# Attention and two MoE layers on one core: a buffer of its own for the scaled last weight, the softmax reciprocals through the landing buffers, and another order of the planned work

## The chip, the cores and the metric

One core of a Trainium2 chip runs the whole program. The metric is the device time of one execution in microseconds (us), and each number for a kernel is the median of several executions.

The five engines of the core go by short names: PE is TensorE (matmuls; PEld are its weight loads), DVE is VectorE, ACT is ScalarE, POOL is GpSimd and SP is SyncE, which here only issues DMAs. A DMA issued by SP or POOL waits in that engine's instruction queue, in order, until the buffer that it writes is free; the transfer itself then runs beside the engines.

## The reference

Attention over 4 batches, 12 heads, 448 positions and head size 64, whose output goes through two dense layers:

```python
scores = cap * np.tanh(q @ k.T / sqrt(64) / cap)          # per batch and head
attn   = exp(scores - max) / (sum + 1e-9)
x      = (attn @ v)                                        # -> [1792 tokens, 768]
h      = ((x @ w1) * (x @ w2)) @ w3 @ w_out                # 768 -> 1024 -> 1024 -> 768
h      = h @ w_in                                          # second layer, 768 -> 1024
solu   = h * softmax(h);  ln = (solu - mean) / sqrt(var + 1e-6) * g_ln
out    = ln @ w_out2                                       # 1024 -> 768
```

## The kernel before

**Arithmetic.** Operands are split into a high and a low part (`split`: ACT copies the high part, DVE subtracts), and a product is three matmuls. The weights arrive as 64-bit words: SP loads a piece into a landing buffer (`landing`, tag `ld`, three of them), and `convert` turns it into 32-bit numbers with three DVE instructions, L168 to L170, into one of two buffers with the tag `cv`.

**Stages.** While attention runs (24 pairs of heads), PE is given other matmuls between the attention's. First is the fold: w3 times w_out (L375), then that times w_in (L393), stored to `w_dr` and loaded back in 16 pieces through the landing buffers (`load34`). Then come the gated products `ab` (L601), w1 and w2 of the first layer against the attention's results `xs`, for batches 0 and 1, and after attention's end for batches 2 and 3. From 582 us on there are two stages of block products (`seven`, L731): the folded matrix, then the last weight `wout2` against the second layer's activations.

**The planned work beside it.** Everything that feeds these matmuls stands in one list (`Ahead`, filled in order by `plan_...`). An item has up to three steps: a load, a first step and a rest; loads run up to three items ahead, and two items are taken for each half pair of heads. The items that matter here:

- `plan_w(f)`, f from 0 to 7: three pieces of w1 and w2, landed, converted and split into `wt`, of which there are two at a time. The slot for f is free when the products of f - 2 are done.
- `plan_last(f)`: two halves of the last weight. Each is landed and converted into a `cv` buffer, scaled in place by `g_ln` on ACT (L532) and stored from that buffer to `wg_dr` by SP (L533).
- `plan_x(b)`: three parts of two head pairs each. POOL loads the reciprocals of the softmax sums, spread over 64 partitions each, into the one buffer `rb` (L456); DVE multiplies the attention's output `xr` by it (L464); `split` makes `xs` of that. There are three `xr` buffers, and part (b, i) uses the buffer of part (b - 1, i).

The list's order before is w0, x of batch 0, w1, x of batch 1, w2, w3, then w4 to w7 each followed by four halves of the last weight, and the x of batches 2 and 3 behind all that. A scheduler then orders each engine's instructions from this: the list sets priority and, among loads that want a landing buffer, who gets it; work whose own buffers are free may run much earlier than its place in the list. At the end of each pair, ACT copies the outputs out of PSUM (L303, two buffers `x`), and POOL moves them into `xr` (L304).

Of the kernel before, what the change touches and what calls it, by code (L numbers as in the profile page):

```python
# [10 lines left out]
F32 = mybir.dt.float32  # L11
F32R = mybir.dt.float32r
U32 = mybir.dt.uint32
AF = mybir.ActivationFunctionType
# [5 lines left out]
P = 128  # L20
B, H, S, D = 4, 12, 448, 64
NPAIR = H // 2
NT = B * S
DM = H * D
DF = 1024
NC, NF = DM // P, DF // P
HALF = 512
# [12 lines left out]
LANDS = 3  # L40
# [5 lines left out]
def raw(ap):  # L46

    return ap.bitcast(F32)
# [50 lines left out]
def attention_moe_solu(ctx: ExitStack, tc: tile.TileContext, q, k, v, cap, w12, w3t, wo, win, wout2, g_ln, out):  # L99
# [9 lines left out]
    pe, act, dve, pool, sync = nc.tensor, nc.scalar, nc.vector, nc.gpsimd, nc.sync  # L109
# [18 lines left out]
    gt = const.tile([P, NF], F32, name="gt")  # L128
    conv = ctx.enter_context(tc.tile_pool(name="conv", bufs=1))
# [18 lines left out]
    lands, cvs = {}, {}  # L148

    def landing(i, src, n, kind):  # L150
        t = conv.tile([P, 2 * HALF], U32, tag="ld", bufs=LANDS, name=f"ld{i}")
        lands[i] = t[:, :n].bitcast(kind)
        dst = lands[i]
        if len(src.shape) == 3:
            dst = dst.rearrange("p (a b) -> p a b", a=src.shape[1])
        elif len(src.shape) == 4:
            dst = dst.rearrange("p (a b c) -> p a b c", a=src.shape[1], b=src.shape[2])
            for g in range(src.shape[1]):
                sync.dma_start(out=dst[:, g], in_=src[:, g])
            return  # L160
        sync.dma_start(out=dst, in_=src)

    def convert(i, n):

        d = lands.pop(i).rearrange("p (n w) -> p n w", w=2)
        lo, hi = d[:, :, 0], d[:, :, 1]
        x = conv.tile([P, HALF], U32, tag="cv", bufs=2, name=f"cv{i}")[:, :n]
        dve.tensor_scalar(x, hi, 5, 2, ALU.logical_shift_left, ALU.logical_shift_right)  # L168
        dve.scalar_tensor_tensor(x, hi, 0xC0000000, x, ALU.bitwise_and, ALU.bitwise_or)  # L169
        dve.scalar_tensor_tensor(x, lo, 29, x, ALU.logical_shift_right, ALU.bitwise_or)  # L170
        cvs[i] = x.bitcast(F32)

    def split(th, tl, x):
        act.copy(th, x)
        dve.tensor_tensor(tl, x, raw(th), ALU.subtract)  # L175
# [11 lines left out]
    landed, ready, parts, outs, xr, stored, inv = {}, {}, {}, {}, {}, set(), [None]  # L187
# [215 lines left out]
    wt, xs, rb, fin = {}, {}, {}, set()  # L403
# [14 lines left out]
    def plan_w(f):  # L418
        for i in range(3):
            plan64(("w", f, i), w12[f, i], HALF, lambda i=i: slot12(f, i), lambda: free12(f))  # L420

    def plan_again(f):
        def load():
            for i in range(3):
                slot12(f, i)
            sync.dma_start(out=raw(wt[f]), in_=w12_dr[f - NF])
        for i in range(3):
            ahead.add(("w", f, i), load if i == 0 else (lambda: None), lambda: None, lambda: None, None, lambda: free12(f))

    def place_x(b, c):  # L430

        n = b * NC + c
        if n < W3 or n >= 2 * W3:
            return w3p.tile([P, 2, HALF], F32R, tag="w3", bufs=W3, name=f"xs{b}_{c}")[:, :, :S]
        return place["x"].tile([P, 2, S], F32R, tag="xs", bufs=W3, name=f"xs{b}_{c}")

    def free_x(b, part):
        if (b, part) not in stored:
            return False
        if b == 0:  # L440
            return pos[0] >= STAGE1 + (HALFWAY if part else 0)
        return (pos[0] >= STAGE1 + HALFWAY if (b, part) == (1, 0) else "x" in place) and (b < 3 or (NF - 1, 0) in fin)

    def plan_x(b):
        for part in range(NPAIR // 2):
            if (b, part) == (B - 1, NPAIR // 2 - 1):

                plan_again(NF + 2)
            i = len(ahead.items)
            pairs = slice(2 * part, 2 * part + 2)  # L450

            def load(i=i, pairs=pairs):
                rb[i] = conv.tile([P, 2, S], F32, tag="rb", name=f"rb{i}")
                for j in range(2):
                    row = r_dr[b].rearrange("(n j) s -> j n s", j=2)[j:j + 1, pairs]
                    pool.dma_start(out=rb[i][j * D:(j + 1) * D], in_=row.to_broadcast([D, 2, S]))  # L456

            def first(i=i, part=part):

                for c in (2 * part, 2 * part + 1):  # L460
                    xs[b, c] = place_x(b, c)
                one = raw(xs[b, 2 * part + 1][:, 0, :1])
                pool.memset(one, 1.0)
                dve.scalar_tensor_tensor(xr[b, part], xr[b, part], one, rb.pop(i), ALU.mult, ALU.mult)  # L464

            def rest(part=part):
                x = xr.pop((b, part))
                for i in range(2):
                    split(xs[b, 2 * part + i][:, 0], xs[b, 2 * part + i][:, 1], x[:, i])
            ahead.add(("x", b, part), load, first, rest, None, lambda part=part: free_x(b, part))  # L470
# [55 lines left out]
    def plan_last(f):  # L526
        for u in range(2):
            i = len(ahead.items)

            def rest(i=i, u=u):  # L530
                t = cvs.pop(i)
                act.activation(t, t, AF.Copy, scale=gt[:, f:f + 1])  # L532
                sync.dma_start(out=wg_dr[f, u], in_=t)  # L533
            ahead.add(("g", f, u), lambda i=i, u=u: landing(i, wout2[f, u].bitcast(U32), DM, U32), lambda i=i: convert(i, DM // 2), rest)

    plan_w(0)
    plan_x(0)
    plan_w(1)
    plan_x(1)
    for f in range(2, NF):  # L540
        plan_w(f)
        if f >= 4:
            plan_last(2 * f - 8)
            plan_last(2 * f - 7)
    plan_again(NF)
    plan_again(NF + 1)
    plan_x(2)
    plan_x(3)
    for i_ in range(NF // 2):
        for part in range(2):  # L550
# [124 lines left out]
    for s in range(2 * NP + 1):  # L675
        n, u = divmod(s, 2)
# [149 lines left out]
    w, wg = DM // 2, {}  # L826
# [102 lines left out]
```

## Time and profile before

| | us |
|---|---|
| median of three runs | 840.35 (839.52 to 841.06) |
| the profiled execution, its own time | 839.32 |
| its span, first to last instruction | 837.5 |
| PE busy | 819.4 (98%) |
| DVE busy | 596.7 (71%) |
| ACT busy | 482.9 (58%) |
| POOL busy | 77.5 (9%) |
| mean granted TensorE clock | 0.993 |

The profile is of one execution. Starts are microseconds from the first instruction. A wait is idle time of an engine just ahead of an instruction, with what ended it. Matmuls overlap and their ends are modelled, so the busy share of PE flatters it a little; what counts is how closely the matmuls follow one another.

### The profile page before, as it was taken

How to read it: one execution, taken by the hardware profiler on the slowest of the kernel's cores; microseconds unless marked ns; L12 is line 12 of the kernel's file. 1: busy time of each engine (PE TensorE's matmuls, PEld its weight loads, DVE VectorE, ACT ScalarE, POOL GpSimd, SP SyncE). 2: the span in 40 equal slices, each digit the busy share in tenths (PEclk: the TensorE clock that was granted, in tenths of full speed). 3: DMA queues.
4: the chain of work that ended last, by engine and by line, in shares of the span. 5: the costliest groups of instructions: out<-in, count | busy, mean ns of one | idle time of the engine just before them, and what ended most of it. 6: DMA issues, size and time to landing. Idle time of an engine off the chain costs nothing.

```text
span 837.5 us, 12335 instructions
## 1 busy us (share of the span) xinstructions
PE 819.4 (98%) x4392; PEld 686.6 (82%) x4392; DVE 596.7 (71%) x1068; ACT 482.9 (58%) x745; POOL 77.5 (9%) x147
## 2 busy tenths in 40 slices
PE   6999999999999999999899999999999999999998
PEld 4677898667677787777778899999888888999997
DVE  7999986896866688786883554342987876995452
ACT  4698866698787676766762121112555655863341
POOL 1012001112111111011112000000000000000000
PEclk8999999999999999999999999999999999999999
DMA  8777775777786366668679699992533325744211
GB/s 262 261 222 224 225 212 176 215 256 249 233 244 189 83 231 220 209 218 279 213 231 295 215 368 390 359 330 73 191 101 126 101 101 189 228 184 155 88 64 75
DMA packets 92573, 173.48 MB, mean 207 GB/s; under 512 B 9696, under 2 KB 63200, under 8 KB 90464
## 3 DMA queue, kind: packets, MB, share of 16 engines
q1 hardware_dynamic: 87520, 161.51, 57.8%
q0 software_dynamic: 4992, 11.19, 5.3%
q8 instruction: 34, 0.56, 0.3%
q14 instruction: 27, 0.22, 0.1%
HBM read 116.40 MB, written 50.68 MB: 199 GB/s over the span
## 4 chain that ended last, share of the span: by engine, by line
PE 62%; DMA 11%; DVE 11%; issue 10%; ACT 5%; POOL 1%; SPq 0%; DVEq 0%; ACTq 0%; POOLq 0%
PE ab L601 21%; PE u L731 16%; PE v L731 8%; PE o L286 5%; PE y L731 4%; PE f L393 3%; DVE cv L170 2%; PE sc L245 2%; DVE cv L169 2%; ACT sc L254 2%; DMA inv<-x 1%; PE tp L801 1%; DMA ld<-w_dr 1%; DMA wg_dr<-cv 1%; DMA ld<-in_wo 1%
## 5 line engine op out<-in xcount | busy, mean ns | idle before, releaser
L601 PE MATMUL ab<-xs,wt 128*128 128x448 f32 x1152 | 242.4, 369 | 1.5 <-DMA wt<-w_dr 0.9
L601 PEld LDWEIGHTS ab<-xs,wt 128*128 128x128 f32 x1152 | 216.2, 189 | 25.5 <-issue 6.1
L286 PE MATMUL o<-hi,v 128*66 128x448 f32 (+1 forms) x396 | 95.3, 371 | 0.9 <-ACT x L303 0.9
L255 ACT ACTIVATE p<-sc,capt 128x896 f32<-128x896 f32 x96 | 87.8, 921 | 12.0 <-DVE lo L270 9.9
L254 ACT ACTIVATE sc<-sc,qscale 128x896 f32<-128x896 f32 x96 | 84.4, 884 | 14.6 <-PE sc L245 13.3
L270 DVE TENSOR_TENSOR lo<-p,hi 128x896 fp32r<-128x896 f32 x66 | 71.4, 1084 | 17.5 <-ACT hi L266 17.5
L731 PE MATMUL u<-ws,a 128*128 128x512 f32 x336 | 82.1, 394 | 0.0
L375 PEld LDWEIGHTS f<-w,w_o 128*128 128x128 f32 x576 | 72.8, 191 | 9.8 <-issue 5.1
L375 PE MATMUL f<-w,w_o 128*128 128x256 f32 x576 | 78.8, 288 | 0.8 <-DVE w_o L175 0.3
L731 PEld LDWEIGHTS u<-ws,a 128*128 128x128 f32 x336 | 62.9, 187 | 14.7
L393 PE MATMUL f<-w_i,w 128*128 128x512 f32 x288 | 71.7, 397 | 0.7 <-DVE w L175 0.4
L266 ACT CAST hi<-p 128x896 fp32r<-128x896 f32 x66 | 62.1, 946 | 11.5 <-PE o L286 11.3
L393 PEld LDWEIGHTS f<-w_i,w 128*128 128x128 f32 x288 | 52.8, 188 | 16.2 <-issue 2.8
L731 PE MATMUL u<-wg,c 128*128 128x384 f32 x336 | 65.4, 340 | 0.0
L286 PEld LDWEIGHTS o<-hi,v 128*66 128x66 f32 (+1 forms) x396 | 42.8, 135 | 26.5 <-issue 10.1
L605 ACT COPY a<-ab 128x448 f32<-128x448 f32 x32 | 17.1, 534 | 74.8 <-PE ab L601 68.4
L731 PEld LDWEIGHTS u<-wg,c 128*128 128x128 f32 x336 | 58.3, 188 | 0.1
L168 DVE TENSOR_SCALAR cv<-ld 128x512 uint32<-128x512 uint32 (+1 forms) x80 | 32.4, 408 | 32.2 <-DMA wg_dr<-cv 13.5
L169 DVE SCALAR_TENSOR_TENSOR cv<-ld,cv 128x512 uint32<-128x512 uint32 (+1 forms) x80 | 52.2, 658 | 0.8
L170 DVE SCALAR_TENSOR_TENSOR cv<-ld,cv 128x512 uint32<-128x512 uint32 (+1 forms) x80 | 52.2, 658 | 0.7
L304 POOL DMA_DIRECT2D xr<-x x48 | 27.5, 576 | 267.8 <-ACT x L303 267.4
L286 PE MATMUL o<-lo,v 128*66 128x448 f32 x132 | 47.6, 365 | 0.0
(129 smaller groups left out, 1228.3 us busy)
## 6 DMA issues: line engine op xcount, KB each, us to landing
ld<-in_w SPq DMA_DIRECT2D x24, 512.0 KB, 4.7
w_dr<-wt SPq DMA_DIRECT2D x8, 1536.0 KB, 7.3
wt<-w_dr SPq DMA_DIRECT2D x8, 1536.0 KB, 8.5
ld<-in_w3t SPq DMA_DIRECT2D x16, 512.0 KB, 4.2
ab_dr<-abs SPq DMA_DIRECT2D x32, 224.0 KB, 5.2
ldab<-ab_dr SPq DMA_DIRECT2D x14, 512.0 KB, 3.9
c_dr<-e SPq DMA_DIRECT2D x14, 512.0 KB, 2.7
ldc<-c_dr SPq DMA_DIRECT2D x14, 512.0 KB, 3.7
```

What stands on the lines that cost most here:

```text
L168: dve.tensor_scalar(x, hi, 5, 2, ALU.logical_shift_left, ALU.logical_shift_right)
L169: dve.scalar_tensor_tensor(x, hi, 0xC0000000, x, ALU.bitwise_and, ALU.bitwise_or)
L170: dve.scalar_tensor_tensor(x, lo, 29, x, ALU.logical_shift_right, ALU.bitwise_or)
L254: act.activation(sc[:, :w, :S], sc[:, :w, :S], AF.Tanh, scale=qscale)
L255: act.activation(p, sc[:, :w, :S], AF.Exp, scale=capt)
L266: act.copy(hi, p)
L270: dve.tensor_tensor(lo, p, raw(hi), ALU.subtract)
L286: product_.append(pe.matmul(outs[n, j][:v_.shape[-1], :S], v_, t[rows, j if c < 3 else 0], **flags))
L375: pe.matmul(f[:, :QW], lw[:, a], rw[:, e], start=(g == 0 and m == 0), stop=(g == NF - 1 and m == 2))
L393: pe.matmul(f, w34[:, a, c, :], rw[:, e], start=(c == 0 and m == 0), stop=(c == NC - 1 and m == 2))
L601: pe.matmul(pp[f, b, i][:, :S], w[:, u], xs[b, c][:, e], start=(c == 0 and m == 0), stop=(c == NC - 1 and m == 2))
L731: pe.matmul(bank, a[m][:, x, k * P:(k + 1) * P], wb[m][:, e, k, :], start=(first and k == 0 and i == 0), stop=(k == NF // 2 - 1 and i == 2 ...
```

## The change

Three things change. The scaled half of the last weight is written by ACT into a buffer of its own (tag `wg`, two of them) and stored from there. The reciprocals land in a landing buffer (tag `ld`) in place of `rb`, which is gone. And the list is put in another order: halves of the last weight stand behind each w from w2 on (w2 g0, w3 g1, w4 g2, w5 g3, w6 g4 g6, w7 g5 g7, where g is `plan_last`), and the three parts of batch 2's x stand behind w4, w5 and w6.

```diff
-    def plan_x(b):
-        for part in range(NPAIR // 2):
+    def plan_x(b, parts=range(NPAIR // 2)):
+        for part in parts:
...
             def load(i=i, pairs=pairs):
-                rb[i] = conv.tile([P, 2, S], F32, tag="rb", name=f"rb{i}")
+                rb[i] = conv.tile([P, 2 * HALF], U32, tag="ld", bufs=LANDS, name=f"rb{i}")[:, :2 * S].bitcast(F32).rearrange("p (n s) -> p n s", n=2)
...
             def rest(i=i, u=u):
-                t = cvs.pop(i)
-                act.activation(t, t, AF.Copy, scale=gt[:, f:f + 1])
+                t = conv.tile([P, DM // 2], F32, tag="wg", bufs=2, name=f"wg{f}_{u}")
+                act.activation(t, cvs.pop(i), AF.Copy, scale=gt[:, f:f + 1])
                 sync.dma_start(out=wg_dr[f, u], in_=t)
...
     for f in range(2, NF):
         plan_w(f)
-        if f >= 4:
-            plan_last(2 * f - 8)
-            plan_last(2 * f - 7)
+        plan_last(f - 2)
+        if f >= 6:
+            plan_last(f)
+        if 4 <= f < 7:
+            plan_x(2, (f - 4,))
     plan_again(NF)
     plan_again(NF + 1)
-    plan_x(2)
     plan_x(3)
```

## Rows read from the trace of the kernel before

**Rows 1.** The page's head: span, then busy time, share and instructions by engine.
```profile
span 837.5 us, 12335 instructions
PE 819.4 (98%) x4392; PEld 686.6 (82%) x4392; DVE 596.7 (71%) x1068; ACT 482.9 (58%) x745; POOL 77.5 (9%) x147
```
**Rows 2.** Busy time by stretch: bounds, length, engines (instructions), granted clock, DMA share, GB/s.
```profile
160.00:240.00 80.00, 78.20 (x388) 56.30 (x388) 64.03 (x105) 64.59 (x92) 10.86 (x20) 1.00 0.80 253
400.00:420.00 20.00, 18.67 (x93) 15.03 (x95) 15.96 (x27) 14.43 (x21) 2.79 (x5) 0.91 0.74 242
480.00:560.00 80.00, 80.00 (x398) 74.44 (x397) 35.75 (x77) 15.10 (x21) 0.00 (x0) 1.00 1.04 367
```
**Rows 3.** PE's waits, 340 to 480 us: total us, times, longest.
```profile
PE sc L245 <- ACT p L255: 2.7, 2, 2.5
PE ab L601 <- DMA wt<-w_dr: 0.9, 1, 0.9
PE ab L601 <- ACT a L605: 0.6, 1, 0.6
```
**Rows 4.** Timeline, 388 to 402 us: start, length, engine, line, operation, [idle before <- releaser].
```profile
390.41 0.36 DVE L168 TENSOR_SCALAR cv<-ld 128x384 uint32<-128x384 uint32 x1 [3.88 <-DMA wg_dr<-cv]
...
392.00 0.62 ACT L532 ACTIVATE cv<-cv,gt 128x384 f32<-128x384 f32 x1 [3.89 <-DVE cv L170]
...
401.33 0.47 PE L245 MATMUL sc<-ql,kh 64*128 64x448 f32 x2 [2.46 <-ACT p L255]
```
**Rows 5.** All engines' waits, 340 to 480 us.
```profile
ACT cv L532 <- DVE cv L170: 24.0, 9, 3.9
...
DVE cv L168 <- DMA wg_dr<-cv: 13.5, 9, 3.9
```
**Rows 6.** The tensor wg_dr: engine, operation, count, duration ns, starts; then landing times.
```profile
L533 SPq DMA_DIRECT2D wg_dr<-cv x16: 319/382/1243, 347.4 to 451.2; - x16
...
DMA to landing us min/median/max: 3.3/5.9/9.2
```
**Rows 7.** Stretches as in rows 2, the gated products' instructions alone.
```profile
402.60:406.10 3.50, 3.31 (x9) 2.96 (x10) 0.00 (x0) 0.00 (x0) 0.51 0.95 278
413.20:416.70 3.50, 3.50 (x18) 3.25 (x18) 0.00 (x0) 0.00 (x0) 1.00 0.88 339
```
**Rows 8.** Line L456, the reciprocals' loads: durations, starts, landing times.
```profile
L456 POOL DMA_DIRECT2D rb<-r_dr x24: 587/604/693, 60.0 to 467.1; - x24
...
DMA to landing us min/median/max: 3.3/4.6/9.3
```
**Rows 9.** Timeline, 143 to 188 us: the first x part, and the outputs that need its buffer.
```profile
144.75 1.14 DVE L464 SCALAR_TENSOR_TENSOR xr<-xr,xs,rb 128x896 f32<-128x896 f32 x1
...
154.56 0.54 POOL L304 DMA_DIRECT2D xr<-x  x1
...
187.64 0.96 ACT L303 COPY x<-o 65x448 f32<-65x448 f32 x2
```
**Rows 10.** Timeline, 175 to 184 us: landing buffers change hands while the fold runs.
```profile
175.98 0.33 SPq L161 DMA_DIRECT2D ld<-in_w  x1
...
176.58 0.33 SPq L161 DMA_DIRECT2D ld<-w_dr  x1
...
180.54 0.84 ACT L174 CAST w<-ld 128x768 fp32r<-128x768 f32 x1 [0.32 <-DMA ld<-w_dr]
...
182.88 0.95 DVE L175 TENSOR_TENSOR w<-ld,w 128x768 fp32r<-128x768 f32 x1
```
**Rows 11.** All engines' waits, 160 to 262 us: those on the landing buffers' loads.
```profile
ACT w L174 <- DMA ld<-w_dr: 7.7, 4, 4.4
DVE cv L168 <- DMA ld<-in_w: 7.7, 4, 2.5
```
**Rows 12.** Timeline, 341 to 366 us: w4's split, and the first output for batch 3.
```profile
341.10 1.15 ACT L174 CAST wt<-cv 128x512 fp32r<-128x512 f32 x2 [0.38 <-PE ab L601]
...
365.51 1.05 POOL L304 DMA_DIRECT2D xr<-x  x2 [2.10 <-ACT x L303]
```

## The prediction

> **What bounds the kernel now.** I read the page's head first: PE is busy for 819.4 of 837.5 us [rows 1], so a change that adds and removes no matmul can only win back PE's gaps or open new ones. The busy time by stretch says where gaps are. From 480 us on PE has none, 80.0 of 80.0 us [rows 2], so a microsecond that PE loses or saves before that is a microsecond of the whole. While attention runs it has a few: 1.8 us in 160 to 240, 1.3 us in 400 to 420 [rows 2]. In that second stretch the granted clock is 0.91 as well, so some of its matmuls ran at the lower of the two levels.
>
> PE's own waits from 340 to 480 us name the gaps where the last weight is prepared [rows 3]: 2.5 us once for an Exp on ACT, 0.6 us for a copy on ACT, 0.9 us for the load of a first-layer weight. The timeline follows the first one back [rows 4]. At 390.41 DVE begins the conversion of a half of the last weight after 3.88 us of waiting for a store to `wg_dr`; at 392.00 ACT begins the scaling of that half after 3.89 us of waiting for the conversion. Both engines work in order, so the Tanh and Exp of scores that were already there stood behind that on ACT, and at 401.33 PE starts new scores after an idle 2.46 us. Nor is it one accident: DVE waited nine times for such a store, 13.5 us in all, and ACT nine times for such a conversion, 24.0 us [rows 5].
>
> **The buffer of its own.** Scaled in place, a `cv` buffer stays taken until its store has landed, 5.9 us in the median and up to 9.2 [rows 6], and there are two. With `wg` it is free when ACT has read it. No instruction is added: ACT's scaling and SP's store have the same sizes and counts, at the same cost. What goes is DVE's 13.5 us of waiting and most of ACT's 24.0; they count only through PE. There I take the 2.46 us [rows 4], the copy's 0.6 us [rows 3], which I put down to the same queueing on ACT, and the slow clock behind the first gap: from 402.6 to 406.1 it was 0.51, with 9 matmuls where a later stretch of the same length has 18 [rows 7], so 3.5 x (1 - 0.51) = 1.7 us. Together 4.8 us; from below the bound is 0, if other waits of the same chain end there. The load's 0.9 us stays: it starts when the last products of batch 1 give up its slot, whatever the rest does.
>
> The change adds a wait: ACT's write of `wg` waits for the store two halves earlier, and behind it on ACT stand the attention's Tanh and Exp. Up to f = 5 the new order has two halves per weight, and the next two only after another weight's slot has come free, so the stores are done. Behind w6 and w7 stand four halves each, so four writes can meet a store under way. The nearest price is DVE's own wait, 13.5 / 9 = 1.5 us [rows 5]. I take 0, because ACT comes to the buffer one conversion later than DVE came to its own; the upper end is 4 x 1.5 = 6.0 us on ACT, of which PE sees a part.
>
> **The other places in the list.** Halves begin behind w2 in place of w4, so the same 16 conversions lie over a longer stretch; cost nothing, as w2 and w3 wait there for their slots anyway. Batch 2's x stands behind w4, w5 and w6. Before, it was far behind in the list and still ran early, as soon as its reciprocals were there. Now its first part comes after w4, whose pieces are split from 341.1, and after two halves; with 4.6 us of landing [rows 8] and 1.1 us of multiplication [rows 9] I put its end at about 356. The next user of its `xr` buffer is POOL's move of batch 3's first output at 365.51 [rows 12]; behind that move on POOL stand the sums' moves and further reciprocals. Nine microseconds cover it, so 0; if they were gone, ACT's output copies would come to wait.
>
> **The landing buffers.** This is what the change pays. `rb` was free, so the first reciprocals were loaded at 60.0 [rows 8] and multiplied at 144.75, long before their place in the list. Now all twelve parts stand in the ring of three landing buffers, in the list's order: the first behind the last piece of w0, loaded at 175.98, the next three before and behind w1. The twelve pairs of POOL loads, their sizes and the twelve multiplications are unchanged; what moves is the time, by some 35 us for the first part.
>
> Two things hang on it. The `xr` buffer of batch 1's first outputs comes free later: POOL's moves of 154.56 shift to about 187, and the copies at 187.64 [rows 9], which can't be made until those moves have landed, by some 3 us. And the fold's pieces stand in the same ring and are needed at once. The piece loaded at 176.58 is split at 180.54, 0.32 us after ACT began to wait for it, and its subtraction ends at 183.8 [rows 10]; that buffer now goes to the reciprocals first. ACT waited 7.7 us for such pieces from 160 to 262 us, and DVE as long for pieces of w1 and w2 [rows 11]: the ring is full.
>
> No row shows reciprocals in a landing buffer. By the piece of 176.58 a buffer is held for 7.2 us, of three, so each of the four parts shifts the ring by 2.4 us: 9.6 us for the last of the fold's pieces, if PE has nothing else. From below it is 0, if attention's matmuls fill PE. A gain is excluded here: a buffer is taken away and none given. Between these I go by this stretch: 7.7 us of ACT's waiting for pieces stood beside 1.8 us of PE idle [rows 2, 11], so 0.23 of a delay reaches PE: 9.6 x 0.23 = 2.2 us.
>
> A rule speaks against the move too. The Trainium skill (SBUF — State Buffer, "SBUF: two separate sides") says that a DMA issued by POOL cannot write its descriptors while certain DVE instructions hold a port that the two share, and gives 3.1 us in place of 0.62 for such a DMA. The reciprocals' loads now fall into a stretch where DVE is busy for 64 of 80 us [rows 2]. By the page, four loads longer by 2.5 us would, as an estimate, add 4 x 2.5 / 3 x 0.23 = 0.8 us. The trace doesn't bear that out: 24 such issues took 587 to 693 ns [rows 8], with DVE as busy.
>
> **The sum.** The profiled execution took 839.32 us, 1.8 more than its span. 839.32 - 4.8 + 2.2 = 836.7 us. The median of the runs shown lies 1.0 above it, so I forecast 837.7 us.
>
> **Rivals.** *The wait moves to ACT* (chance 0.23). One of the four writes behind w6 and w7 meets its store, and a gap like the one at 401 comes back there, without the slow clock: 840.35 - 4.8 + 2.5 + 2.2 = 840.2 us. For it speaks that four halves in a row are what ended so before; against it, that ACT has a conversion's time more.
>
> *The fold starves* (0.29). PE's idle follows the ring in full, between 176 and 235 us: 840.35 - 4.8 + 9.6 = 845.2 us. It decides from the point where over 6.5 of the 9.6 us reach PE (4.8 won plus the 1.7 us that can be told from no change). For it: PE works ACT and DVE hard there, 64.6 and 64.0 of 80 us [rows 2], so attention can't run ahead freely. Against it: PE hid most of such delays so far. A worse form is in this chance: reciprocals ready at 60.0 would take a landing buffer then and hold it until 144.75; the list's order should keep that from happening.
>
> **How the numbers follow.** The forecast's case has 0.48, with its own range of 835.6 (nothing lost in the ring) to 838.6. Two executions of this kernel differ by about 0.2%, 1.7 us, and no less can be told from no change. By the cases: faster 0.48, same 0.23, slower 0.29. The range goes from 834.0, for small gaps beyond the three that I counted, to 845.2, the starved fold's.
>
> **What would show it.** Right: DVE's waits for stores of `wg_dr` gone, ACT's waits for conversions of these halves well under 24.0 us, no PE gap over 1 us between 340 and 460 us and a clock of 1.00 there; the first multiplication by reciprocals near 182; PE idle in 160 to 240 us at about 4 us in place of 1.8. Wrong: a gap of the same kind after 410, with ACT waiting for a store; PE idle of over 8 us in 160 to 240; or a fold whose early loads, before 144 us, come later than now. A scheduler orders all of it anew, so single gaps may move for reasons that none of these steps holds.

## The result, and the profile after

The kernel after takes 845.58 us in the median (842.30 to 846.72), the kernel before, run beside it, 839.90 us (838.02 to 841.68). The ratio is 1.007, with a 95% interval of 1.0052 to 1.0088: slower, where faster was forecast. The time lies 0.4 us above the top of the range. It is the time of the rival "the fold starves", 845.2 us, and most of what follows asks how far its reason was the right one. In the code of after the lines from 543 on stand one lower: the gated products are L602, and a half of the last weight is scaled at L532 into `wg`.

The page's head, as in [rows 1]: the span is 6.4 us longer than before, PE's busy time 1.2 us more, so in the net most of the loss is PE standing still. (The net hides that some matmuls ran slower and others faster than before, as the clock shows below.)

```profile
span 843.9 us, 12369 instructions
PE 820.6 (97%) x4392; PEld 687.6 (81%) x4392; DVE 597.8 (71%) x1068; ACT 483.3 (57%) x745; POOL 76.7 (9%) x147
```

Busy time by stretch in after, the columns as in [rows 2]. The first three lines answer to those of before; then come two stretches in the fold, the whole of the gated products beside attention, and what follows it.

```profile
160.00:240.00 80.00, 73.62 (x353) 52.58 (x352) 62.68 (x102) 62.59 (x90) 14.11 (x27) 0.94 0.74 234
400.00:420.00 20.00, 20.00 (x109) 16.46 (x108) 16.80 (x32) 16.23 (x24) 3.56 (x6) 1.00 0.62 210
480.00:560.00 80.00, 78.82 (x391) 72.98 (x390) 37.94 (x84) 13.98 (x19) 0.00 (x0) 1.00 1.02 363
196.20:199.60 3.40, 3.28 (x11) 2.07 (x12) 0.96 (x1) 3.40 (x6) 0.00 (x0) 0.50 0.24 91
226.90:233.70 6.80, 5.26 (x19) 3.98 (x19) 6.23 (x10) 6.80 (x13) 1.06 (x2) 0.50 0.66 215
280.00:460.00 180.00, 180.00 (x962) 144.13 (x961) 136.30 (x246) 125.24 (x181) 27.75 (x53) 1.00 0.67 228
```

The same view of before for the stretch that [rows 2] doesn't hold:

```profile
280.00:460.00 180.00, 176.60 (x925) 140.85 (x925) 131.55 (x237) 118.69 (x172) 26.36 (x49) 0.99 0.70 228
```

So there is a gain and a larger loss. From 280 to 460 us PE's idle went from 3.4 us to none, and the clock from 0.99 to 1.00. From 160 to 240 us the idle went from 1.8 to 6.4 us, and the clock from 1.00 to 0.94: two stretches, of 3.4 and 6.8 us, ran at a granted clock of 0.50, the lower level of 1.2 GHz.

What this cost the fold is read best from the second product's line (L393; durations in ns, then first and last start). In before and in after:

```profile
L393 PE MATMUL f<-w_i,w x288: 387/389/506, 145.0 to 262.7; 128*128 128x512 f32 x144
```
```profile
L393 PE MATMUL f<-w_i,w x288: 387/389/793, 145.8 to 271.6; 128*128 128x512 f32 x144
```

From its first to its last matmul the fold took 117.7 us before and 125.8 us after, 8.1 more. (It also begins 0.8 us later, where no reciprocals have been loaded yet; in e1 and e8 below, with the same ring, it begins at 145.1 and 144.9.) The stretch table gives about as much: 4.6 us more of idle, and 3.28 + 5.26 us of matmuls at half the clock, worth some 4.3 us, 8.9 together.

Which work was last there? The chain of waits of before, 150 to 270 us (start, length, what), goes from one landing buffer's load to the next:

```profile
176.58 3.94 DMA ld<-w_dr
...
194.65 3.73 DMA ld<-in_w
...
202.21 5.41 DMA ld<-in_w
...
208.96 7.68 DMA ld<-w_dr
```

The same view of after, 165 to 240 us:

```profile
173.33 5.73 DMA rb<-r_dr
...
183.41 1.23 POOL xr L304 x2
...
185.17 8.23 DMA xr<-x
...
200.27 3.73 DMA rb<-r_dr
...
214.43 6.62 DMA inv<-x
```

Two things are to be seen. In before the chain already ran through the landing ring, though PE hid most of its waits. In after the reciprocals are links of it: their landing (5.73 us), then the moves that could not be issued before the multiplication and the split behind it, and those moves' own landing (8.23 us), for which ACT's copies wait. The last line is POOL's move of softmax sums; it stood on POOL behind a second set of such moves.

The timeline of after has the two places where this reaches PE, around 194 us and around 227 us:

```profile
183.41 2.28 POOL L304 DMA_DIRECT2D xr<-x  x4 [1.30 <-DVE xs L175]
...
193.39 0.96 ACT L303 COPY x<-o 65x448 f32<-65x448 f32 x2 [4.71 <-DMA xr<-x]
...
193.97 0.62 PE L286 MATMUL o<-hi,v 128*66 128x448 f32 x2 [0.63 <-ACT x L303]
...
196.32 0.74 PE L245 MATMUL sc<-ql,kh 64*128 64x448 f32 x2 [1.54 <-ACT p L255]
...
221.17 0.23 DVE L315 TENSOR_SCALAR inv<-inv,guard 112x16 f32<-112x16 f32 x1 [1.67 <-DMA inv<-x]
...
222.02 8.19 SPq L161 DMA_DIRECT2D ld<-w_dr  x4
222.03 0.62 ACT L174 CAST wt<-cv 128x512 fp32r<-128x512 f32 x1 [5.34 <-DVE cv L170]
...
226.21 0.73 PE L393 MATMUL f<-w_i,w 128*128 128x512 f32 x2 [2.20 <-ACT w L174]
...
228.49 0.74 PE L245 MATMUL sc<-ql,kh 64*128 64x448 f32 x2 [1.54 <-ACT p L255]
```

The first is the order of the `xr` buffer: the moves stood at 154.56 before [rows 9], now they come after the first multiplication. The second is the ring: the fold's piece that before was loaded at 208.96 and split at 216.66 is loaded at 222.02, as soon as a conversion of a first-layer weight has given its buffer back, and split at 225.34. DVE had that conversion standing behind its wait for the softmax sums (1.67 us), and ACT waited 5.34 us for it. Each time ACT, which works in order, waits with the attention's Exp behind it, so PE loses the fold's matmuls and the scores together, and behind each gap the clock is low.

One more loss had not been foreseen. The timeline of after around the last two loads of first-layer weights:

```profile
467.66 0.33 SPq L426 DMA_DIRECT2D wt<-w_dr  x1
...
477.26 36.51 PE L602 MATMUL ab<-xs,wt 128*128 128x448 f32 x180 [2.33 <-DMA wt<-w_dr]
...
506.51 0.33 SPq L426 DMA_DIRECT2D wt<-w_dr  x1
...
514.95 1.25 PE L602 MATMUL ab<-xs,wt 128*128 128x448 f32 x5 [1.18 <-DMA wt<-w_dr]
```

These gaps sum to 3.5 us where before had one of 0.9 [rows 3]. Together: 8.1 (fold) + 0.8 (ahead of it) - 3.4 - 1.7 (idle and clock from 280 to 460) + 2.7 (these loads) = 6.5 us, and the spans differ by 6.4.

### The profile page after: what moved, and what is told of

It is laid out like the page before. It is cut to its first block, busy times and chain, and to the rows that moved or that the text cites. A ratio compares the mean times of both kernels' runs of the same rounds, so it can differ in the third digit from the quotient of the medians.

```text
span 843.9 us, 12369 instructions
## 1 busy us (share of the span) xinstructions
PE 820.6 (97%) x4392; PEld 687.6 (81%) x4392; DVE 597.8 (71%) x1068; ACT 483.3 (57%) x745; POOL 76.7 (9%) x147
## 4 chain that ended last, share of the span: by engine, by line
PE 72%; issue 10%; DMA 9%; DVE 6%; ACT 2%; POOL 1%; SPq 0%; DVEq 0%; POOLq 0%; ACTq 0%
PE ab L602 26%; PE u L732 16%; PE v L732 8%; PE o L286 8%; PE y L732 4%; PE sc L245 3%; PE f L393 3%; DMA wt<-w_dr 2%; DMA inv<-x 2%; PE tp L802 1%; DMA rb<-r_dr 1%; PE sc L241 1%; DVE cv L170 1%; DMA xr<-x 1%; POOL xr L304 1%
## 5 line engine op out<-in xcount | busy, mean ns | idle before, releaser
L602 PE MATMUL ab<-xs,wt 128*128 128x448 f32 x1152 | 241.2, 367 | 3.5 <-DMA wt<-w_dr 3.5
L602 PEld LDWEIGHTS ab<-xs,wt 128*128 128x128 f32 x1152 | 214.9, 188 | 27.3 <-issue 9.3
L393 PE MATMUL f<-w_i,w 128*128 128x512 f32 x288 | 71.7, 400 | 2.6 <-ACT w L174 2.2
L393 PEld LDWEIGHTS f<-w_i,w 128*128 128x128 f32 x288 | 54.0, 191 | 17.9 <-ACT w L174 2.6
L610 DVE TENSOR_TENSOR abs<-ab,a 128x448 f32<-128x448 f32 x32 | 19.9, 621 | 37.8 <-PE ab L602 17.8
```

Source lines behind the costliest of these rows:

```text
L393: pe.matmul(f, w34[:, a, c, :], rw[:, e], start=(c == 0 and m == 0), stop=(c == NC - 1 and m == 2))
L602: pe.matmul(pp[f, b, i][:, :S], w[:, u], xs[b, c][:, e], start=(c == 0 and m == 0), stop=(c == NC - 1 and m == 2))
```

## The experiments

**Theory:** the reciprocals in the landing ring cost about 8 us in the fold, and the rest of the change wins some 5 us. **Rivals:** the list's new order costs the time by itself; the buffer `wg` is worth nothing or costs; the scratch memory given to `wg` matters. Where `rb` and `wg` stand side by side there isn't room for both, so in those kernels `wg` lies in another pool, paid with one of six scratch buffers (`ts`); e11 prices that. The table has the medians, the ratio to the kernel before run beside each, the fold's second product from first to last matmul, and PE's busy time in the 180 us from 280 to 460. The last two columns are of one profiled execution each; that of e1 and e9 was the shortest among its kernel's runs, that of e3, e7, e10 and e11 the longest, so small differences between them say little.

| kernel | median us | ratio (95%) | fold us | PE 280–460 |
|---|---|---|---|---|
| before | 839.90 | | 117.7 | 176.60 |
| after | 845.58 | 1.0070 (1.0052–1.0088) | 125.8 | 180.00 |
| e1 ring and order, no `wg` | 846.58 | 1.0096 (1.0078–1.0114) | 125.7 | 179.10 |
| e2 order alone | 848.15 | 1.0111 (1.0094–1.0127) | 117.6 | 171.25 |
| e3 `wg` alone | 835.94 | 0.9956 (0.9936–0.9976) | 118.1 | 177.88 |
| e4 order and `wg`, no ring | 840.26 | 1.0020 (0.9995–1.0044) | 116.1 | 176.16 |
| e5 after, ring of four | 837.80 | 1.0002 (0.9982–1.0023) | 118.4 | 178.40 |
| e6 after, `rb` for batches 0 and 1 | 835.44 | 0.9960 (0.9944–0.9975) | 118.0 | 180.00 |
| e7 e4, batch 2's x at its old place | 838.37 | 0.9980 (0.9961–0.9999) | 116.9 | 176.47 |
| e8 ring and `wg`, old order | 858.42 | 1.0228 (1.0210–1.0245) | 125.1 | 176.81 |
| e9 after, `rb` for the first part alone | 838.28 | 1.0004 (0.9985–1.0024) | 118.2 | 180.00 |
| e10 after, `rb` for the other five parts | 839.10 | 1.0006 (0.9983–1.0029) | 121.9 | 179.13 |
| e11 after, `wg` in the other pool | 843.66 | 1.0070 (1.0047–1.0092) | 125.3 | 180.00 |
| e12 e6, halves in fours as before | 839.61 | 1.0010 (0.9992–1.0028) | 116.8 | 177.84 |

**e1, ring and new order without the buffer of its own.**

```diff
-                t = conv.tile([P, DM // 2], F32, tag="wg", bufs=2, name=f"wg{f}_{u}")
-                act.activation(t, cvs.pop(i), AF.Copy, scale=gt[:, f:f + 1])
+                t = cvs.pop(i)
+                act.activation(t, t, AF.Copy, scale=gt[:, f:f + 1])
```

> The changed kernel with the last weight scaled in place again (no wg). Theory A (the ring): the loss of 8 us between 145 and 272 us is all from the reciprocals in the landing buffers, and the gain of 6 us after that is all from wg; then the fold ends near 272 us as in the changed kernel, waits of DVE for stores of wg_dr come back (about 10 us), and the time is 848 to 852 us. Theory B (the order): the gain is from the last weight's halves being spread, not from wg; then about 845.5 us as the changed kernel.

846.58 us, 1.0 above after in the medians and 0.26%, some 2 us, by the ratios. All engines' waits, 280 to 500 us (total, times, longest):

```profile
DVE cv L168 <- DMA wg_dr<-cv: 16.8, 10, 3.6
```

DVE waits more for the stores than before (16.8 us against the 13.5 of [rows 5]), and yet PE is busy for 179.10 of 180 us. Spread over more of the list, the same waits hardly reach PE; in this order, with the ring, `wg` itself is worth 1 to 2 us, hardly to be told from nothing (the two intervals overlap). The fold is as long as in after, so `wg` has nothing to do with the loss.

**e2, the new order alone** (`rb` kept, scaled in place).

```diff
 before, and:
-        if f >= 4:
-            plan_last(2 * f - 8)
-            plan_last(2 * f - 7)
+        plan_last(f - 2)
+        if f >= 6:
+            plan_last(f)
+        if 4 <= f < 7:
+            plan_x(2, (f - 4,))
...
-    plan_x(2)
```

> The kernel before with the list's new order alone (rb kept, scaled in place). Theory A: the fold ends near 263 us as before; no ring loss; the halves of the last weight are spread, so at most part of the gaps near 400 goes: 837 to 840.5 us. Theory B: the order alone makes the whole gain of 6 us: 834 to 836 us. Theory C (the order costs time in the fold or in the loads of w at 474 and 513 us): 842 us or more.

848.15 us, slower than after, with a fold as short as before's. So the order isn't what lengthens the fold, but alone it opens another gap. The timeline of e2:

```profile
322.28 1.26 POOL L456 DMA_DIRECT2D rb<-r_dr  x2 [3.13 <-DMA r_dr<-inv]
...
330.96 1.15 DVE L464 SCALAR_TENSOR_TENSOR xr<-xr,xs,rb 128x896 f32<-128x896 f32 x1 [7.01 <-DMA rb<-r_dr]
...
333.67 1.49 PE L602 MATMUL ab<-xs,wt 128*128 128x448 f32 x3 [3.47 <-ACT a L606]
```

With a buffer of their own batch 2's reciprocals are loaded as soon as they exist, and DVE, in order, stands 7.01 us in front of that multiplication. ACT waits for its result, and behind that on ACT is the copy `a` that gives a PSUM buffer back, for which PE waits 3.47 us. The kernel before has `rb` too, and there the same multiplication, at 324.07, waits only 1.86 us; so the private buffer makes this wait possible, and the new order makes it long.

**e3, the buffer of its own alone**, in the old order.

```diff
 before, and:
-                t = cvs.pop(i)
-                act.activation(t, t, AF.Copy, scale=gt[:, f:f + 1])
+                t = place["ab"].tile([P, DM // 2], F32, tag="wg", bufs=2, name=f"wg{f}_{u}")
+                act.activation(t, cvs.pop(i), AF.Copy, scale=gt[:, f:f + 1])
...
 tag="ts": bufs=6 -> 5
```

> The kernel before with the buffers wg alone: rb kept, the list in its old order; wg lies in the pool of the gated products' results, and the buffers of the sums (ts) are five for six to make room. Theory A: DVE's 13.5 us of waits for stores gone, no gap over 1 us between 340 and 460 us, fold end near 263 us: 834 to 837 us. Theory B: the four halves in a row keep the gaps, ACT waits for wg in place of DVE: 839 to 841 us.

835.94 us, ratio 0.9956: faster, by about 3.7 us. ACT now waits for the stores (280 to 500 us):

```profile
ACT wg L532 <- DMA wg_dr<-wg: 11.5, 4, 3.3
```

So the wait did move to ACT, as the prediction's rival "the wait moves to ACT" had it, but not with the full price: PE's idle from 280 to 460 is 2.1 us, where before had 3.4, and that in the longest of this kernel's ten runs (838.45 us).

**e4, order and `wg`, reciprocals in `rb`.**

```diff
 after, and:
-                rb[i] = conv.tile([P, 2 * HALF], U32, tag="ld", ...)
+                rb[i] = conv.tile([P, 2, S], F32, tag="rb", name=f"rb{i}")
-                t = conv.tile([P, DM // 2], F32, tag="wg", ...)
+                t = place["ab"].tile([P, DM // 2], F32, tag="wg", bufs=2, name=f"wg{f}_{u}")
...
 tag="ts": bufs=6 -> 5
```

> The changed kernel with rb back for the reciprocals: wg and the new order kept (wg in the pool of the gated products' results, ts five for six). Theory A: fold end near 263 us, waits for stores gone: 833 to 836 us, 9 to 12 us under the changed kernel. Theory C (the order costs, not the ring): 842 us or more.

840.26 us, not to be told from before. The fold is 9.7 us shorter than in after: the ring is what lengthened it. But the gap of e2 is there too, smaller (the timeline of e4):

```profile
327.12 1.15 DVE L464 SCALAR_TENSOR_TENSOR xr<-xr,xs,rb 128x896 f32<-128x896 f32 x1 [4.45 <-DMA rb<-r_dr]
...
329.83 0.87 PE L602 MATMUL ab<-xs,wt 128*128 128x448 f32 x3 [1.96 <-ACT a L606]
```

From 280 to 460 PE is idle for 3.8 us, with the clock at 0.99, where after had none. So the ring also does some good, most likely by keeping batch 2's reciprocals in the list's order: e6 below, with only those of batches 0 and 1 out of the ring, has no such gap.

**e5, after with a ring of four** (still three items ahead; paid with two scratch buffers).

```diff
 after with wg in the other pool, and:
-LANDS = 3
+LANDS = 4
...
-    ahead = Ahead(LANDS)
+    ahead = Ahead(3)
...
 tag="ts": bufs=6 -> 4
```

> The changed kernel with four landing buffers for three, loads still three items ahead (wg in the pool of the gated products' results, ts four for six to make room). Theory A1 (the ring is too short for the fold's pieces and the reciprocals): the gap at 222 us and the one at 193 us go, the fold ends near 263 us instead of 272: 836 to 840 us. Theory A2 (the reciprocals come late by their place in the list, however many buffers there are): the first multiplication stays near 180 us, the outputs' copies wait near 193 us, the fold ends at 268 us or later: 842 us or more.

837.80 us, no different from before; the fold takes 118.4 us. The cost of the reciprocals is that of a buffer in the ring, not of their transfers: those are the same here, and their multiplication is late as well (the first at 170.8, in after at 179.19). No run gave the kernel before a ring of four, so what a longer ring wins by itself is not known; e4 and e6 show the cost of the reciprocals without it.

**e6, the ring from batch 2 on.**

```diff
 after with wg in the other pool (ts 5), and:
-                rb[i] = conv.tile([P, 2 * HALF], U32, tag="ld", ...)
+                rb[i] = (conv.tile([P, 2, S], F32, tag="rb", name=f"rb{i}") if b < 2 else
+                         conv.tile([P, 2 * HALF], U32, tag="ld", ...))
```

> The changed kernel with rb back for the reciprocals of batches 0 and 1 alone; those of batches 2 and 3 stay in the landing buffers (wg in the pool of the gated products' results, ts five for six). Theory A (only batches 0 and 1 in the ring cost, through the fold): fold end near 263 us, no gap in 180 to 240 us over 1.5 us; with the clean stretch from 300 to 460 us that the changed kernel has, 834 to 838 us. Rival (the clean stretch came from the fold's delay): a gap of 2 us or more near 327 us, behind a wait of DVE for batch 2's reciprocals: 840 to 844 us.

835.44 us (835.38 to 837.61), ratio 0.996: faster than both kernels, 9 us (by the ratios) to 10 us (by the medians) under after. The fold's line and two stretches:

```profile
L393 PE MATMUL f<-w_i,w x288: 387/389/505, 144.5 to 262.5; 128*128 128x512 f32 x144
```
```profile
160.00:240.00 80.00, 77.72 (x388) 56.14 (x385) 64.47 (x106) 64.96 (x93) 10.46 (x20) 1.00 0.82 254
...
280.00:460.00 180.00, 180.00 (x955) 145.39 (x954) 134.95 (x244) 120.97 (x175) 27.83 (x53) 1.00 0.68 232
```

Both halves are there: before's fold and after's gated products. e3 gets as far by `wg` alone; the two can't be told apart by these runs.

**e7, e4 with batch 2's x at its old place in the list.**

```diff
 e4, and:
-        if 4 <= f < 7:
-            plan_x(2, (f - 4,))
...
+    plan_x(2)
     plan_x(3)
```

> All but the ring, and batch 2's x back at its old place in the list: rb and wg, the halves of the last weight behind w2 to w7. Theory D (the gap at 327 us of the runs with the new order and rb is from batch 2's x having a higher place, so that DVE is made to wait for its reciprocals): no such gap, 834 to 837 us. Rival (it is from the halves being moved ahead to w2 and w3): the gap stays, 839 to 842 us.

838.37 us, and the gap near 327 stays. PE's waits from 280 to 500 us have it as

```profile
PE ab L601 <- ACT a L605: 3.1, 1, 3.1
```

PE is idle for 3.5 us from 280 to 460, and the clock is 0.83 from 320 to 340. It is not x's place in the list that makes it, since in `rb` that x runs ahead of its place anyway. What remains is the halves that now stand there, or how the scheduler placed the load; these runs don't settle which.

**e8, ring and `wg` in the old order.**

```diff
 after, and the list of before:
-        plan_last(f - 2)
-        if f >= 6:
-            plan_last(f)
-        if 4 <= f < 7:
-            plan_x(2, (f - 4,))
+        if f >= 4:
+            plan_last(2 * f - 8)
+            plan_last(2 * f - 7)
...
+    plan_x(2)
     plan_x(3)
```

> The ring and wg with the list in its old order. Theory A: the fold's loss of 8 us is there as in the changed kernel. Batch 2's x now gets its landing buffers only behind all weights, after 436 us, while batch 3's first outputs want its xr buffer at 366 us: attention stops there for some 60 us with PE only partly filled, 860 us or more. Rival (loads with a lower place still get in between): 843 to 847 us, and then the new order wasn't needed for the ring.

858.42 us, the slowest of all. The fold is as long as in after; then, at the end of attention, in the timeline and by stretch:

```profile
438.03 1.15 DVE L464 SCALAR_TENSOR_TENSOR xr<-xr,xs,rb 128x896 f32<-128x896 f32 x1 [2.21 <-DMA rb<-r_dr]
...
489.55 10.75 PE L601 MATMUL ab<-xs,wt 128*128 128x448 f32 x44 [3.78 <-DMA wt<-w_dr]
...
496.96 1.15 DVE L464 SCALAR_TENSOR_TENSOR xr<-xr,xs,rb 128x896 f32<-128x896 f32 x1 [10.52 <-DMA rb<-r_dr]
```
```profile
440.00:480.00 40.00, 31.45 (x151) 22.11 (x150) 19.76 (x29) 21.67 (x35) 11.32 (x26) 0.92 0.40 113
480.00:500.00 20.00, 16.22 (x71) 14.54 (x71) 4.06 (x8) 1.57 (x3) 1.77 (x3) 0.90 0.60 182
```

In the ring an x comes no earlier than its place in the list, and at the old place batches 2 and 3 come after all the weights. PE loses 12.3 us of these 60. So with the ring the new order is worth some 13 us (0.0228 less 0.0070). e8 puts the halves back as well; that it is batch 2's x that was missing is read from these waits; no run with the ring moved it alone.

**e9 and e10, which of the reciprocals.** Two causes were proposed for the fold: the first part's late multiplication, which holds an `xr` buffer (the gap at 194), and the pieces standing behind reciprocals (the gap at 227). e9 takes the first part of batch 0 out of the ring, e10 the other five parts of batches 0 and 1.

```diff
 e6, with for e9:
-... if b < 2 else ...
+... if (b, pairs.start) == (0, 0) else ...
 and for e10:
-... if b < 2 else ...
+... if b < 2 and (b, pairs.start) != (0, 0) else ...
```

> The changed kernel with rb back for the very first part of x alone (batch 0, part 0); the other eleven stay in the landing buffers (wg and ts placed as in e6). If the two gaps in the fold have two causes: the first multiplication is back near 145 us, the outputs' copies at 193 us no longer wait and that gap (about 3.5 us with its slow clock) goes, the gap at 222 us (about 5 us) stays; fold end near 268 us, 841 to 843 us. If the first gap makes the second (all is one delay): both go, 836 to 838 us.

> The opposite: the first part in a landing buffer, rb for the other five parts of batches 0 and 1. Two causes: the copies at 193 us wait as in the changed kernel, the fold's piece for 222 us lands near 210 us and that gap goes; fold end near 266 us, 838 to 841 us. One delay: both gaps stay, 844 us or more.

> The changed kernel with only what e6, e9 and e10 have in common beside rb: wg in the pool of the gated products' results and five ts buffers for six. All theories: nothing on the path, 844.5 to 846.5 us as the changed kernel; if it is under 842 us, the place of wg and not rb made e6 fast.

e11 is after with only `wg`'s pool changed, so that e9 and e10 differ from it in `rb` alone: 843.66 us, the same ratio as after, with the same gaps. The place of `wg` is no cause. e9 takes 838.28 us and e10 839.10, 5.4 and 4.6 us less than e11. The copy that waits in after, in e9 and in e10:

```profile
186.96 0.97 ACT L303 COPY x<-o 65x448 f32<-65x448 f32 x2
```
```profile
193.19 0.96 ACT L303 COPY x<-o 65x448 f32<-65x448 f32 x2 [4.38 <-DMA xr<-x]
```

And the load of the fold's piece that after made at 222.02 and e11 at 221.00, in e9 and in e10:

```profile
215.99 8.11 SPq L161 DMA_DIRECT2D ld<-w_dr  x4
```
```profile
212.43 4.43 SPq L161 DMA_DIRECT2D ld<-w_dr  x2
```

So each does what its mechanism says: in e9 the copy doesn't wait, in e10 it waits as in after, but the piece comes 8.6 us earlier. In e9 the gap of the ring is still there (idle of 1.0 and 1.5 us at 219 to 222), but no low clock follows it, and the piece comes 5.0 us earlier, as the whole chain begins sooner; hence each alone wins over half of what e6 wins (by the ratios 0.66% and 0.64%, of 1.10%), and the two overlap. How the rest divides can't be read from these traces: the profiled execution of e9 is the shortest of its ten (834.46), that of e10 the longest (842.69), so their folds, 118.2 and 121.9 us, are not those of the median.

**e12, e6 with the halves in fours behind w4 to w7.**

```diff
 e6, and:
-        plan_last(f - 2)
-        if f >= 6:
-            plan_last(f)
+        if f >= 4:
+            plan_last(2 * f - 8)
+            plan_last(2 * f - 7)
```

> e6 with the halves of the last weight back in fours behind w4 to w7; batch 2's x stays between, in landing buffers, and wg stays. If the spread of the halves is worth something by itself: a gap or two near 400 us comes back and the time is 837 to 840 us. If wg alone takes the gaps at 400 us away: 834 to 836.5 us, as e6.

839.61 us, 4.2 above e6. The timeline of e12:

```profile
417.03 0.62 ACT L533 ACTIVATE wg<-cv,gt 128x384 f32<-128x384 f32 x1 [3.31 <-DMA wg_dr<-wg]
...
422.00 0.47 PE L245 MATMUL sc<-ql,kh 64*128 64x448 f32 x2 [0.95 <-ACT p L255]
```

This is that same rival, "the wait moves to ACT", in its pure form: with four halves in a row ACT waits for a store, and PE stands 0.95 us for the Exp behind it. From 280 to 460 us PE is idle for 2.2 us, where e6 has none; the rest of the 4.2 us has no place in these traces. In after, where they are spread, ACT waits for stores for 4.4 us in all and none of it reaches PE.

## Why the prediction was wrong, point by point

**The ring: the place was right, the size was not.** The term was 9.6 x 0.23 = 2.2 us; the fold became 8.1 us longer, and by e4, e5 and e6 the ring alone did that. The counting held: four parts fell into 160 to 240 us (loaded at 172.7, 199.7, 205.5 and 222.9), and each kept its buffer for 5.6 to 7.6 us, where 7.2 was taken. The step that failed is the factor 0.23, the overlap by which PE was to hide most of the delay. It divided PE's idle by ACT's waits for the fold's pieces in the stretch of before, as if a longer wait were hidden in the same proportion; 8.1 of 9.6 is 0.84. Nor is the wait that it scaled the one that grew. ACT's waits for pieces, 7.7 us in before [rows 11], are none in after, and in their place, from 160 to 240 us, stand

```profile
ACT wt L174 <- DVE cv L170: 7.5, 3, 5.3
...
ACT x L303 <- DMA xr<-x: 4.7, 1, 4.7
```

The chain of waits of before, which the prediction didn't read for this stretch, already ran from landing to landing, so there was little room left for more. ACT carries the pieces' splits and the attention's Exp in one order, so its longer waits took both of PE's sources at once. And the term had no clock in it, where half of the loss, some 4.3 us, was matmuls at 0.50.

That the rival's 845.2 us came within 0.4 us is in part luck. Its 9.6 us were PE's idle alone, and PE's idle in that stretch grew by 4.6; the low clock made up most of the rest, and two losses that no rival had, 0.8 us ahead of the fold and 2.7 us behind attention, filled the sum. In the profiled execution the forecast's sum of 836.7 us was missed by 8.9 (845.63): 5.9 in the ring's term, 2.7 and 0.8 in those two, less 0.3 by which the gain was larger.

**The copies: a shift that was seen and not priced.** Moves "to about 187" (they came at 183.41) and copies "by some 3 us" later (by 5.8) stood in the text and in no sum. In e9, which undoes this and takes one part out of the ring, 5.4 us come back.

**The gain: right in place and size, but not a term of `wg` alone.** 4.8 us were forecast between 340 and 460; from 280 to 460 the trace gives 3.4 + 1.7 = 5.1. The signs named for it held: no wait of DVE for a store of `wg_dr`, no gap there, a clock of 1.00. In the old order the credit to `wg` stands: e3 wins 3.7 us by it (2.0 to 5.4). But in the new order with the ring, taking `wg` away costs only 1 to 2 us (e1), as there the spread halves leave PE busy for 179.10 of 180 us without it. The order was put down at nothing; alone it costs some 9 us (e2), beside `wg` some 5 (e4 against e3), and with the ring and `wg` it wins some 13 (e8). e12 puts the spread of the halves at about 4 us beside `wg`. The parts aren't worth the same in each other's company, and a sum of terms priced one by one couldn't show that.

**ACT's new wait at nothing:** held in after, where the halves are spread, and did not hold where they stand in fours (e12, and in part e3).

**Batch 2's x at nothing:** held in after (180.00 of 180 us). The text had it as a move that costs nothing; by e8's waits the ring needs it.

**The weight's load "stays" at 0.9 us:** it became 3.5 us in two gaps. In after the first load lands 9.5 us after its issue (467.66 to 477.2), where before took 8.1; four loads for the sums of weight blocks stand just ahead of it on SP, at 461.50, which before had from 440 to 451 and again from 483. The second is issued at 506.51, 11.7 us later than before's load of the same weight, on SP behind stores of those sums' results. That these are the causes is argued from the order alone; no run took them away.

**The rule on POOL's DMAs.** The reciprocals' loads in after took 587 to 931 ns (L456):

```profile
L456 POOL DMA_DIRECT2D rb<-r_dr x24: 587/602/931, 172.7 to 467.7; - x24
```

The Trainium skill (SBUF — State Buffer, "SBUF: two separate sides") gives 3.1 us for such a DMA issued against the port that DVE holds. The longest is 931 ns, where before's was 693 [rows 8]; nothing near 3.1 us shows, and the loss in the fold is not this. (The prediction's estimate by that rule counted four loads; each part has two, 24 for twelve parts, so four parts are eight, and by its own way of reckoning the estimate would have been 1.5 us.)

**What would have told.** The prediction set "idle of over 8 us in 160 to 240" as the sign of failure. It came to 6.4, neither 4 nor 8: the sign counted idle and not the matmuls at half the clock, which made up the rest.

## What to carry to other kernels

Before you move a load into a shared ring, read the chain of waits in the stretch where the ring is used: if the chain runs through the ring's landings, expect each buffer taken to cost most of its hold (here 8.1 us for four holds that come to 9.6), however little idle stood there before. Price every shift that you name, and look for what queues behind it on the in-order engine that feeds several users. Where two parts of a change attack the same wait, what one wins depends on the other, so credit the sum once. Keep a shared buffer for the work whose order you want held (batch 2) and a private one for what could run early (batches 0 and 1).

## What the runs showed of the hardware

PE's idle of about 2 us was followed by the low clock in some places and not in others. In after the gaps of 0.63 and 1.54 us at 194 to 196 were followed by 3.4 us at a granted clock of 0.50, and those of 2.20 and 1.54 us at 226 to 228 by 6.8 us. The gap of 2.33 us at 477 was followed by none: the stretch from 480 to 560 has 1.00. And in e9 the same two gaps at 219 to 222, of 1.0 and 1.5 us, left no mark, with 1.00 throughout 160 to 240:

```profile
160.00:240.00 80.00, 77.45 (x390) 56.53 (x391) 65.22 (x105) 64.99 (x93) 12.30 (x24) 1.00 0.76 249
```

So neither the length of a gap nor a pair of them told here whether the clock would fall, and what does was not tried.
